# A fused retention and SoLU kernel with another written order: where each step stands in the queues, and which engine does it

## The chip, the cores and the metric

The kernel runs on one core of one Trainium2 chip. The time is the device time of one execution in microseconds (us), lower is better. The core has five instruction queues that run side by side: PE (TensorE, matrix products; its weight loads are shown as PEld), DVE (VectorE), ACT (ScalarE), POOL (GpSimd) and SP (SyncE, which here only issues DMA transfers). Each takes its instructions in the order in which they were written, and waits where an operand or a buffer is not ready.

## The reference

Per batch element and head, a causal product with decay (no softmax), and then a feed-forward layer over the joined heads:

```python
# q, k, v: 8 batch elements, 8 heads, 576 tokens, 64 wide, float32
scores = q @ k.T / 8
ret    = scores * gamma_h ** (i - j)         # for i >= j, otherwise 0
x      = (ret @ v), heads joined             # 4608 tokens x 512
h      = x @ w_in                            # 512 -> 1024
e      = exp(h - max(h));  sm = e / sum(e)
solu   = h * sm
ln     = (solu - mean(solu)) / sqrt(var(solu) + 1e-6) * g_ln
out    = ln @ w_out                          # 1024 -> 512
```

## The kernel before, in words

The 4608 tokens are cut into 36 chunks of 128 tokens, in four groups of nine; a group covers two batch elements, with chunks 0, 2, 4, 6 of one, 1, 3, 5, 7 of the other, and a ninth that holds the last 64 tokens of both. Within a batch element a running state (64 x 64 per head) goes from chunk to chunk.

The decay is split into factors of the row and of the column. A chunk runs through these steps (names as in the code):

- `lq`, `lk`, `lv`: SyncE issues loads of 256 KB each (profile lines L271 and L275).
- `cq`, `ck`, `cv`: scale or cast to f16 (tiles q, k, v), on GpSimd, VectorE or ScalarE.
- `tq`: PE transposes q and k into the PSUM tile tp; `eq` copies it to qkT (ScalarE or VectorE, L246). Late chunks use DMA transposes (`kd`, `kq`) instead, in part.
- `sc`: PE makes the scores (L392); `mk`: VectorE masks them into ret (L405).
- `av`, `fs`: PE makes x from ret and v, and adds the state's part (L467, L259); `ex` copies it to xT.
- `kv`: PE makes the chunk's state product kp (L416); `ad`: VectorE adds it to the state, t (L431); `dk`, `d3`: GpSimd scales the state for the next chunk (L443, L455).
- `m1` (`mr` by blocks, for the first two chunks): PE multiplies with w_in into h (L259). `mx`: VectorE's maximum (L523). `xp`: ScalarE's exponential, with its sum. `so`: VectorE's product u (L538), with its sum. For the first five chunks `ce` subtracts the mean.
- `sq`: ScalarE's squares (L564, L566); `ra`, `rp`: the factor rs of the row, small operations.
- `tu`: PE transposes u into lp, `eu` copies it to uT; or `du`, a DMA transpose. `m2`: PE multiplies with w_out into o (L259). `st`: ScalarE scales o by rs, and SyncE stores it.

Beside the chunks: `li` loads a quarter of w_in (512 KB), `wi` casts half a quarter; `lo` loads a quarter of w_out, `wo` scales an eighth by g_ln; `mm` multiplies with ones for the mean of w_out over its rows (tile mean), `mc` copies it into the tile warm, and eight steps `ws` subtract it from w_out, into w_c (L832). From the sixth chunk on `m2` uses w_c in place of w_out, so that `ce` is not needed. `wu` is a filler product on PE whose result nobody reads. The last chunk goes by halves (`hm`, `hx`, `hp`, `ho`, `ht`, `he`, `hq`, `h2`, `hw`).

No scheduler orders the work. A table of 1027 tokens, ORDER, is the program's order: a token `cq:7:v` is the step cq of chunk 7 on VectorE (a is ScalarE, g GpSimd). Each queue gets its instructions in this order. Two more tables, BANKS and SLOTS, say which PSUM bank and which SBUF buffer each step takes; there are four banks beside the two buffers of h, so a step of PE also waits for the reader of what stood in its bank:

```python
    def bank(shape, dtype, name):
        return ps.tile(shape, dtype, tag="b" + next(banks), name=name)
...
    def ws(c, e):
        ENG[e].tensor_tensor(out=T["w_c"][:, c], in0=w_out16[:, c], in1=warm, op=ALU.subtract)
...
    def run(order, base):

        for token in order.split():
            name, n, *more = token.split(":")
...
                step[name](n, *more)
```

Of the kernel before, what the change touches and what calls it, by code (L numbers as in the profile page):

```python
# [19 lines left out]

PLAIN = 5
ORDER = """
c1:0 lk:1 lk:0 lq:1 ck:0:v lq:0 cq:1:g lv:1 gt:0 lq:2 ck:1:v li:2 lv:0 cq:2:g cq:0:v tq:1 lk:2
cv:0:g lv:2 c2:0 tq:0 eq:1:av ck:2:a eq:0:v sc:1 li:0 cv:1:g wu:4:2 li:3 mk:1 li:1 wi:2:0:g lq:4
lv:4 lk:4 kv:0 wi:2:1:a lq:3 ad:0 sc:0 lk:3 cv:2:g tq:2 lv:3 eq:2:a av:1 mk:0 ex:1:a kv:1 ad:1
d3:0 av:0 ex:0:v sc:2 wi:0:0:a mr:1:2 dk:1 wi:0:1:g kv:2 mk:2 ad:2 wi:3:1:v wi:3:0:a mr:0:2
wi:1:1:v dk:0 wi:1:0:a lk:5 lq:5 mr:0:0 mr:1:0 mr:1:3 dk:2 mr:1:1 cq:4:g mx:1 mr:0:1 av:2 fs:2
ck:4:g mr:0:3 cv:4:g ex:2:a cq:3:g tq:4 mx:0 d3:1 xp:1 so:1 d3:2 wu:1:3 ce:1 wu:5:4 cv:3:g ck:5:g
eq:4:a cq:5:g sc:4 ck:3:a m1:2 xp:0 lv:5 mk:4 kv:4 tq:3 sq:1 kv:3 lk:6 lq:6 av:4 lv:6 so:0 ad:3
ra:1:g dk:3 ad:4 eq:3:a fs:4 tu:1 sc:3 ex:4:a ce:0 eu:1:a tq:5 d3:4 lo:0 cv:5:g lo:2 rp:1 lo:3  # L30
mx:2 eq:5:a xp:2 lo:1 cq:6:g m1:4 lv:8 mk:3 wu:2:1 ck:6:a cv:6:g tu:0 mx:4 sc:5 av:3 mk:5 eu:0:a
xp:4 fs:3 av:5 tq:6 kv:5 so:2 ex:3:a wo:0:a wo:1:g fs:5 kv:6 lk:8 m1:3 so:4 ce:2 eq:6:a ad:6
wo:4:g lq:7 lq:8 ex:5:a tu:2 sc:6 lk:7 m1:5 wo:6:g ce:4 mk:6 lq:13 wo:7:g wo:5:a d3:3 tu:4 lv:7
eu:2:a wo:2:a av:6 dk:6 wo:3:a mm:0 sq:2 dk:4 cv:8:g sq:4 mx:3 lq:9 eu:4:v m2:0 fs:6 ad:5 sq:0
ck:8:a mx:5 ra:0:v cq:7:v ra:2:v lv:13 mc:0:v lk:11 ck:7:v lq:12 lk:9 lv:10 m2:1 xp:3 lv:9 rp:0
cq:8:g so:3 ws:2:g lq:10 lk:10 ce:3 lq:11 ex:6:a st:0 lv:11 dk:5 ra:4:g st:1 ws:4:v rp:2 lv:16
ws:1:v lv:12 lk:13 tq:7 lk:12 tq:8 m2:2 eq:7:a eq:8:a sc:7 mk:7 xp:5 m1:6 so:5 st:2 rp:4 tu:3
sc:8 m2:4 sq:3 ra:3:v cv:7:g ck:11:a eu:3:a mk:8 cq:9:g av:7 fs:7 ws:7:g d3:5 ck:9:a lq:16 mx:6
kv:7 sq:5 cq:13:g rp:3 m2:3 ex:7:a lv:14 lq:15 ad:7 dk:7 ra:5:v tq:9 ws:5:g ws:3:g st:4 tu:5 m1:7
rp:5 ck:10:g av:8 ws:0:v cv:9:g xp:6 ws:6:v eu:5:a eq:9:va sc:9 so:6 mx:7 st:3 fs:8 ex:8:a m2:5  # L40
lq:21 tu:6 cq:11:g mk:9 cv:11:g m1:8 sq:6 av:9 st:5 cq:10:v kv:9 xp:7 ex:9:a tq:10 cq:12:g eu:6:v
so:7 ad:9 mx:8 eq:10:a ra:6:g cv:10:g sq:7 lq:24 m2:6 sc:10 lk:14 lq:14 xp:8 tu:7 mk:10 m1:9 rp:6
av:10 eu:7:v so:8 kv:10 st:6 ck:12:g ad:10 dk:9 ra:7:g tq:11 mx:9 ex:10:a ck:13:g tq:12 lq:18
tu:8 cv:14:g eq:11:av d3:9 eq:12:a lv:18 m2:7 sq:8 cv:12:g eu:8:a rp:7 sc:11 st:7 ra:8:v lk:16
mk:11 xp:9 lk:15 m1:10 lk:17 kv:11 ad:11 dk:10 av:11 so:9 lq:20 cq:21:g d3:10 kv:12 fs:11 ck:14:a
ad:12 m2:8 lk:18 mx:10 sc:12 lv:15 lk:20 lv:21 rp:8 ex:11:a cq:14:g lq:17 lk:22 tu:9 m1:11 mk:12
cq:16:g sq:9 xp:10 cq:15:g ra:9:v lv:19 st:8 tq:13 eq:13:a eu:9:v av:12 fs:12 tq:14 eq:14:a rp:9
dk:11 so:10 mx:11 m2:9 d3:12 cv:13:g tu:10 ex:12:a sc:13 m1:12 mk:13 st:9 av:13 sc:14 sq:10
eu:10:v xp:11 dk:12 fs:13 mx:12 ex:13:a so:11 xp:12 sq:11 mk:14 m2:10 ra:10:g lv:17 so:12 kv:14
rp:10 m1:13 st:10 ad:14 ck:18:g kv:13 tu:11 d3:11 eu:11:a av:14 ck:16:g ck:15:g ad:13 fs:14 tq:16  # L50
ra:11:v tq:15 du:12 lk:19 cv:16:g cq:17:g rp:11 d3:14 ex:14:a lk:21 d3:13 cv:15:g dk:13 lq:23
lv:24 m2:11 mx:13 dk:14 eq:15:av cv:18:g ck:17:v xp:13 lq:19 sc:15 mk:15 m1:14 eq:16:a av:15
# [36 lines left out]
ht:35:1 he:35:1:v ht:35:0 rp:34 m2:34 he:35:0:v hq:35:1:a rp:33 st:33 ra:35:v h2:35:0 st:34
h2:35:1 rp:35 hw:35:0:a hw:35:1:v  # L90
"""

BANKS = """
0123012031202310231032103021302310321023032031023102103120213120312031201203123031023013021320120312
0312032312013213012312301231302130312032131021301301032012301230130231031201320213021302130231023103
123120123301230103023012103102301320120
# [7 lines left out]
kf 012345102345102345012034513204153240  # L104
qf 012345601234560132564350136405126043
k16 012345012354012543021304532104203451
q16 012340213402134123012301324103104201
vf 012345610234561045301265410365240531
h 010101010101010101010101010101010101
v16 012341023410324012431042301342043120  # L110
qkT 012301230123102310231203120320231023
ret0 012301230123012301230123012301230123
ret1 012301230123012301230123012301230123
t 01230123102310320132013201323012
xT 012301230123012301230123012301230123
s32 0123012301230132013201302
s16 012312032013201320132013201232013
e 01201201201201201201201201201201201
u 01234023140231402314023142013421031
uT 01234102341023410234012340123401230  # L120
o_sb 01230123012301230123012301230123012
"""

# [753 lines left out]
```

## Time and profile before

| | |
|---|---|
| median of 3 runs | 211.23 us (211.11 to 211.67) |
| the profiled execution | 213.29 us |
| its span, from first to last instruction | 211.6 us |
| PE busy | 193.3 us (91%), 3109 matmuls |
| DVE, ACT, POOL busy | 173.3, 169.7, 170.6 us (82%, 80%, 81%) |
| chain that ended last | PE 70%, DMA 10%, issue on SP's queue 8%, DVE 5% |
| DMA | 47.97 MB, mean 227 GB/s |

Busy time on PE is what the profile models from the pipelined matmuls. The chain is followed back from the last instruction, at each step to what released it. A row of waits gives the waiting engine and tile, what it waited for, the sum in us, the count and the longest. A row of the timeline has the start, the length, the engine, line, operation and tiles, and in brackets the idle time ahead of it.

### The profile page before, as it was taken

What the parts mean: (1) busy time and instruction counts of PE and PEld (TensorE: products, weight loads), DVE (VectorE), ACT (ScalarE), POOL (GpSimd) and SP (SyncE); (2) the same over time, 40 slices, a digit from 0 to 9 for tenths busy, and PEclk for the clock granted to TensorE, in tenths of its full rate; (3) what the DMA queues carried; (4) which work ended last, traced back from release to release, by engine and by line L of the source; (5) the groups of instructions that cost most, each with busy time, mean ns of one, the idle gap of its engine ahead of it and who ended that gap; (6) DMA issues with size and microseconds to landing.
All of it is one profiled execution on the core that took longest, in us unless ns stands there. A gap on an engine that the chain in (4) does not pass through costs nothing.

```text
span 211.6 us, 7571 instructions
## 1 busy us (share of the span) xinstructions
PE 193.3 (91%) x3109; PEld 122.1 (58%) x3109; DVE 173.3 (82%) x299; ACT 169.7 (80%) x299; POOL 170.6 (81%) x249
## 2 busy tenths in 40 slices
PE   0468898888999999999999999999999999999992
PEld 0344576555666756676566666667656656555552
DVE  0468999849998969798989898999998999878640
ACT  2135889499988889889699899889989796799861
POOL 3379798679999999869999998789999987378330
PEclk9999999999999999999999999999999999999999
DMA  6999999979798998999999999989999999999734
GB/s 147 308 261 290 239 238 332 229 168 246 177 279 218 303 316 220 213 252 191 266 198 252 242 271 218 228 227 243 197 199 240 201 217 175 173 224 222 183 117 149
DMA packets 111890, 47.97 MB, mean 227 GB/s; under 512 B 95592, under 2 KB 105840, under 8 KB 111856
## 3 DMA queue, kind: packets, MB, share of 16 engines
q1 hardware_dynamic: 111536, 47.33, 97.1%
q8 instruction: 24, 0.39, 0.8%
q10 hardware_dynamic: 320, 0.16, 0.3%
q14 instruction: 10, 0.08, 0.1%
HBM read 32.54 MB, written 9.44 MB: 198 GB/s over the span
## 4 chain that ended last, share of the span: by engine, by line
PE 70%; DMA 10%; SPq 8%; DVE 5%; ACT 3%; issue 2%; POOL 0%; DVEq 0%; ACTq 0%
PE o L259 25%; PE h L259 22%; DMA w_out<-in_moe_w_out_dram 5%; PE tp L254 5%; PE sc L392 4%; SPq L275 3%; DMA w_in<-in_moe_w_in_dram 3%; PE x L259 3%; PE x L467 3%; PE lp L254 3%; SPq L271 2%; DMA vf<-in_v_dram 2%; ACT sq L564 2%; PE kp L416 1%; SPq L800 1%
## 5 line engine op out<-in xcount | busy, mean ns | idle before, releaser
L259 PE MATMUL h<-w_in,xT 128*64 128x512 f16 x560 | 67.3, 380 | 0.5 <-ACT w_in L246 0.3
L259 PE MATMUL o<-w_c,uT 128*64 128x512 f16 x480 | 56.5, 380 | 0.0
L405 DVE TENSOR_TENSOR ret<-sc,tris 128x512 f16<-128x512 f32 x72 | 46.1, 682 | 4.9 <-PE sc L392 4.7
L259 PEld LDWEIGHTS <-xT 128*64 128x64 f16 x576 | 31.0, 110 | 24.6 <-issue 1.4
L523 DVE TENSOR_REDUCE nm<-h 128x1 f32<-128x1024 f32 x35 | 42.5, 1217 | 2.8 <-PE h L259 2.5
L538 DVE SCALAR_TENSOR_TENSOR u<-h,e 128x1024 f16<-128x1024 f32 x35 | 42.5, 1216 | 2.0 <-ACT e L529 1.6
L259 PEld LDWEIGHTS <-uT 128*64 128x64 f16 x560 | 30.4, 111 | 22.6
L529 ACT ACTIVATE e<-h,nm 128x1024 f32<-128x1024 f32 x35 | 39.4, 1127 | 2.1 <-DVE nm L523 1.9
L289 POOL TENSOR_TENSOR v<-vf,small 128x512 f16<-128x512 f32 x34 | 35.4, 1044 | 5.4 <-DMA vf<-in_v_dram 5.3
L300 POOL TENSOR_TENSOR q<-qf,small 128x512 f16<-128x512 f32 x31 | 32.7, 1059 | 7.9 <-DMA qf<-in_q_dram 7.6
L566 ACT ACTIVATE sq<-u,su 128x1024 bf16<-128x1024 f16 x30 | 34.7, 1156 | 0.4 <-DVE u L538 0.2
L443 POOL TENSOR_TENSOR s<-t,small 128x512 f16<-128x512 f32 x32 | 33.5, 1055 | 0.2
L246 ACT COPY qkT<-tp 128x512 f16<-128x512 f16 x46 | 24.7, 595 | 8.4 <-PE tp L254 8.3
L626 ACT ACTIVATE o_sb<-o,rs 128x512 f32<-128x512 f32 x35 | 24.0, 696 | 7.6 <-POOL rs L592 2.3
L246 ACT CAST xT<-x 128x512 f16<-128x512 f32 x31 | 18.3, 594 | 6.6 <-PE x L259 4.9
L592 POOL TENSOR_TENSOR rs<-w,mhalf 128x1 f32<-128x1 f32 x36 | 20.6, 578 | 2.7 <-DVE w L581 1.5
L455 POOL TENSOR_TENSOR s<-t,small 128x256 f32<-128x256 f32 x24 | 15.5, 650 | 1.2 <-DVE t L431 1.1
L467 PE MATMUL x<-ret,v 128*64 128x128 f16 x288 | 14.7, 225 | 1.1 <-DVE ret L405 0.7
L254 PE MATMUL tp<-ident,q 128*64 128x128 f16 x232 | 12.2, 230 | 3.5 <-POOL q L300 3.2
L392 PE MATMUL sc<-qkT 64*128 64x128 f16 x288 | 14.9, 226 | 0.4 <-DVE qkT L246 0.3
L467 PEld LDWEIGHTS <-v 128*64 128x64 f16 x288 | 11.3, 113 | 5.3 <-issue 1.0
L254 PEld LDWEIGHTS <-q 128*64 128x64 f16 x280 | 10.8, 115 | 6.0 <-POOL q L300 3.3
(87 smaller groups left out, 263.1 us busy)
## 6 DMA issues: line engine op xcount, KB each, us to landing
kf<-in_k_dram SPq DMA_DIRECT2D x36, 256.0 KB, 5.2
qf<-in_q_dram SPq DMA_DIRECT2D x36, 256.0 KB, 4.8
vf<-in_v_dram SPq DMA_DIRECT2D x36, 256.0 KB, 5.2
out_dram<-o_sb SPq DMA_DIRECT2D x35, 256.0 KB, 4.2
w_in<-in_moe_w_in_dram SPq DMA_DIRECT2D x4, 512.0 KB, 6.1
w_out<-in_moe_w_out_dram SPq DMA_DIRECT2D x4, 512.0 KB, 8.5
uT<-u SPq DMA_TRANSPOSE x17, 4.4
out_dram<-o_sbh SPq DMA_DIRECT2D x2, 64.0 KB, 1.9
```

The lines of the kernel that those rows point to most:

```text
L246: (engine.copy if engine is nc.scalar else engine.tensor_copy)(out=out, in_=in_)
L254: nc.tensor.transpose(out=out[w], in_=in_[:, w], identity=ident)
L259: nc.tensor.matmul(out=out[w], lhsT=lhsT[:, w], rhs=rhs, start=start, stop=stop, skip_group_check=True,)
L289: engine.tensor_tensor(out=dst, in0=T.pop((key, n)), in1=table.unsqueeze(2).to_broadcast([P, H, D]), op=ALU.mult,)
L300: ENG[e].tensor_tensor(out=dst.rearrange("p (a h) d -> p h a d", h=2), in0=T.pop(("qf", n)).rearrange("p (h a) d -> p h a d", h=2), in1=ta ...
L405: nc.vector.tensor_tensor(out=r, in0=s, in1=m, op=ALU.mult)
L443: nc.gpsimd.tensor_tensor(out=s16, in0=t.unsqueeze(2).to_broadcast([P, 4, 2, D]), in1=gd.unsqueeze(3).to_broadcast([P, 4, 2, D]), op=ALU.mult,
L467: nc.tensor.matmul(out=x[64 * e : 64 * e + 64, hp], lhsT=v16[:, 2 * hp + e], rhs=ret[e][:, hp], start=hp == 0, stop=chunks[n][1] == 0, ski ...
L523: nc.vector.tensor_reduce(out=nm, in_=T["h", n], axis=AX.X, op=ALU.max, negate=True)
L529: nc.scalar.activation(out=e, in_=T["h", n], func=ACT.Exp, bias=T.pop(("nm", n)), accum_out=s)
L538: nc.vector.scalar_tensor_tensor(out=u, in0=T.pop(("h", n)), scalar=-1.0, in1=T.pop(("e", n)), op0=ALU.mult, op1=ALU.mult, accum_out=su,)
L566: nc.scalar.activation(out=s, in_=T.pop(("v", n)), func=ACT.Square, scale=-float(DFF), bias=T.pop(("su", n)), accum_out=ss,)
```

## The change

No function is changed. The three tables are replaced: the same 1027 steps in another order, with other banks and buffers. All 36 chunks keep their path (the same transposes by PE and by DMA). A step may stand on another engine: k's cast is ScalarE's for 19 chunks instead of 13, VectorE's for 3 instead of 6 and GpSimd's for 14 instead of 17; ws is VectorE's seven times instead of four and GpSimd's once instead of four times; half blocks of w_in are cast by ScalarE (4) and GpSimd (4, before 2 and VectorE 2). Chunk 7's q and k are scaled by GpSimd instead of VectorE. The fillers on PE are 13 products instead of 10, most of them ahead of the first product with w_in. One line of ORDER, before and after (the other lines, and the two smaller tables, differ in the same manner):

```diff
-c1:0 lk:1 lk:0 lq:1 ck:0:v lq:0 cq:1:g lv:1 gt:0 lq:2 ck:1:v li:2 lv:0 cq:2:g cq:0:v tq:1 lk:2
+c1:0 lk:1 ck:1:a lq:1 cq:1:g lk:0 lq:0 lq:2 lv:1 cq:0:v tq:1 li:2 lk:2 ck:0:a lv:0 li:0 ck:2:g
```

Three places show what moved. The first is SyncE's queue from the start; kf, qf and vf are loads of k, q and v of a chunk, w_in the loads of w_in. Before:

```order
L275 DMA kf<-in_k_dram 128x8x64 x2
L271 DMA qf<-in_q_dram 128x2x256 x2
L275 DMA vf<-in_v_dram 128x8x64
L271 DMA qf<-in_q_dram 128x2x256
L790 DMA w_in_94<-in_moe_w_in_dram 128x1024
L275 DMA vf<-in_v_dram 128x8x64
L275 DMA kf<-in_k_dram 128x8x64
L275 DMA vf<-in_v_dram 128x8x64
L790 DMA w_in_94<-in_moe_w_in_dram 128x1024 x3
```

After:

```order
L275 DMA kf<-in_k_dram 128x8x64
L271 DMA qf<-in_q_dram 128x2x256
L275 DMA kf<-in_k_dram 128x8x64
L271 DMA qf<-in_q_dram 128x2x256 x2
L275 DMA vf<-in_v_dram 128x8x64
L790 DMA w_in_94<-in_moe_w_in_dram 128x1024
L275 DMA kf<-in_k_dram 128x8x64
L275 DMA vf<-in_v_dram 128x8x64
L790 DMA w_in_94<-in_moe_w_in_dram 128x1024 x2
L275 DMA vf<-in_v_dram 128x8x64
L790 DMA w_in_94<-in_moe_w_in_dram 128x1024
```

The first q goes ahead of the second k, and two of w_in's blocks go ahead of chunk 2's v; the last block is thirteenth in both. Chunks 4, 3, 5 and 6 and then w_out follow in both.

The second place is ScalarE's queue where the last of w_out is scaled (w_out16 from w_out32 and g32), with the squares sq of chunks 0, 2 and 4 and the copy uT of chunk 2. Before:

```order
L246 COPY uT_915<-lp_836 128x1024
L808 ACTIVATE w_out16_97<-w_out32_95,g32_93 128x512 x2
L564 ACTIVATE sq_947,ss_948<-u_775 128x1024
L564 ACTIVATE sq_954,ss_955<-u_818 128x1024
L564 ACTIVATE sq_990,ss_991<-u_560 128x1024
```

After:

```order
L564 ACTIVATE sq_810,ss_811<-u_527 128x1024
L808 ACTIVATE w_out16_97<-w_out32_95,g32_93 128x512 x3
L564 ACTIVATE sq_905,ss_906<-u_777 128x1024
L564 ACTIVATE sq_1008,ss_1009<-u_786 128x1024
L246 COPY uT_1011<-lp_908 128x1024
```

One square goes ahead of the scaling and the copy uT goes behind the other two. The second output product of PE now takes the PSUM bank of the tile lp that this copy reads.

The third place is VectorE's queue at the subtractions w_c (steps `ws`). Before:

```order
L554 TENSOR_SCALAR u_1047<-u_1047,nmu_1055 128x1024
L832 TENSOR_TENSOR w_c_1010<-w_out16_97,warm_89 128x512 x2
L405 TENSOR_TENSOR ret0_1155<-sc0_1145,tris_86 128x512
...
L523 TENSOR_REDUCE nm_1274<-h_1162 128x1
L431 TENSOR_TENSOR t_1315<-kp_1276,s32_1268 128x256
L577 TENSOR_SCALAR w1_1319<-s_1160 128x1
L583 TENSOR_SCALAR w2_1320<-ss_1286,w1_1319 128x1
L832 TENSOR_TENSOR w_c_1010<-w_out16_97,warm_89 128x512 x2
```

After:

```order
L832 TENSOR_TENSOR w_c_1016<-w_out16_97,warm_89 128x512
L549 TENSOR_SCALAR nmu_1147<-su_1103 128x1
L554 TENSOR_SCALAR u_1102<-u_1102,nmu_1147 128x1024
L405 TENSOR_TENSOR ret0_1214<-sc0_1162,tris_86 128x512
...
L523 TENSOR_REDUCE nm_1235<-h_1177 128x1
L832 TENSOR_TENSOR w_c_1016<-w_out16_97,warm_89 128x512 x4
L431 TENSOR_TENSOR t_1367<-kp_1298,s32_1160 128x256
L832 TENSOR_TENSOR w_c_1016<-w_out16_97,warm_89 128x512
L246 COPY uT_1390<-lp_1331 128x1024
```

Four of the subtractions stand between chunk 6's maximum nm and the state sum t of chunk 7, which was ahead of them, and a fifth ahead of the copy uT of chunk 5.

More of the change, by code (lines that the diff above doesn't have):

```diff
@@ L29 @@
[L29 to L40, printed above, removed]
@@ new lines @@
+kv:6 wo:5:a lq:7 m1:3 wo:2:a wo:6:g wo:3:a ad:5 sc:6 wo:7:g m1:5 ce:4 mk:6 ad:6 tu:4 lk:8 dk:4
+sq:2 tu:2 eu:4:v av:6 cv:8:g lq:9 mx:3 lk:7 lq:8 dk:6 lq:13 lv:7 ra:0:v ra:2:v lk:10 lk:9 m2:0
+lv:9 lv:10 mm:0 rp:0 lq:12 cq:7:g sq:4 eu:2:a ck:8:a mc:0:v st:0 mx:5 lk:11 m2:1 lq:10 lk:13
+ck:7:g lv:12 fs:6 cq:8:g rp:2 xp:3 ws:3:g st:1 ws:2:v cv:7:g dk:5 tq:7 lv:13 ex:6:a lk:12 lq:11
+lv:16 lv:11 so:3 ra:4:g eq:7:a m2:2 ws:6:v tq:8 ce:3 xp:5 rp:4 cq:9:g st:2 d3:5 sc:7 eq:8:a
+ck:9:a m1:6 sq:3 tu:3 mk:7 sc:8 so:5 mk:8 mx:6 eu:3:a ws:4:v m2:4 ws:0:v av:7 fs:7 st:4 lv:14
@@ new lines @@
+sc:11 m1:10 mk:11 rp:7 kv:11 d3:10 av:11 ra:8:g rp:8 ad:12 lq:16 fs:11 so:9 ad:11 st:7 ck:14:a
+cq:13:g ck:13:g mx:10 lk:17 ex:11:a lv:19 m2:8 lv:15 dk:11 sq:9 lk:15 st:8 sc:12 lk:20 mk:12
+cq:14:g tu:9 ra:9:v dk:10 lk:22 cq:18:g m1:11 xp:10 tq:13 eu:9:v tq:14 av:12 fs:12 cq:15:g
+eq:13:a lq:17 rp:9 so:10 ex:12:v eq:14:av m2:9 sc:13 lv:21 tu:10 mx:11 mk:13 eu:10:v m1:12 av:13
+sq:10 fs:13 xp:11 d3:12 sc:14 d3:11 so:11 ra:10:g st:9 ck:16:a ex:13:a cq:21:g lv:24 ck:18:g
+cq:16:g mx:12 sq:11 m2:10 kv:14 dk:12 mk:14 lq:23 ad:14 xp:12 so:12 m1:13 ck:15:g tu:11 rp:10
@@ new lines @@
+du:12 cv:15:g lv:17 ra:11:g lq:19 kv:13 st:10 ad:13 d3:14 d3:13 tq:15 lk:21 lk:19 eu:11:a av:14
+mx:13 fs:14 eq:15:av tq:16 ex:14:a m2:11 sq:12 sc:15 dk:13 eq:16:v mk:15 rp:11 xp:13 m1:14
+ck:17:g cq:17:g so:13 av:15 fs:15 cq:23:g st:11 ex:15:a dk:14 kv:15 tq:17 tu:13 sq:13 ad:15 sc:16
+eq:17:a m1:15 mx:14 mk:16 kv:16 xp:14 ra:13:v av:16 eu:13:a fs:16 cv:19:g ex:16:a m2:12 ad:16
+so:14 dk:15 sq:14 dk:16 lv:20 du:14 mx:15 sc:17 lq:20 lk:24 cv:17:g rp:13 m2:13 lv:23 lv:22
+ra:14:g mk:17 xp:15 lq:22 st:13 ck:20:v ra:12:g so:15 tq:18 ck:21:g lk:23 rp:12 rp:14 eq:18:av
@@ new lines @@
+ck:19:a m1:16 cv:18:g av:17 mx:16 st:12 sq:15 xp:16 sc:18 mk:18 so:16 du:16 lk:28 lk:29 lq:25
+fs:17 m2:14 ex:17:a tu:15 st:14 ra:15:v lq:32 cq:19:g tq:19 kv:18 eq:19:a ad:18 m1:17 lq:27
+cq:20:g eu:15:v cv:24:g av:18 mx:17 sc:19 sq:16 m2:15 ex:18:a ck:22:a ck:24:g xp:17 mk:19 kv:19
+tq:20 tq:21 lq:26 rp:15 so:17 eq:20:av cv:21:g cq:22:g m1:18 ad:19 eq:21:av cv:20:g mx:18 cv:23:g
+lk:25 av:19 st:15 sq:17 ex:19:a sc:20 mk:20 xp:18 lq:28 lk:26 so:18 m2:16 tu:17 ck:28:a kv:20
+av:20 ra:16:g du:18 rp:16 eu:17:a dk:18 d3:18 fs:20 st:16 cv:22:g lv:25 ra:17:v lv:26 ck:23:v
@@ new lines @@
+dk:31 av:31 xp:30 d3:30 cv:32:g fs:31 mk:32 lq:35 kq:34 dk:30 d3:31 lv:35 so:30 m1:29 ex:31:a
+cv:33:g du:28 sc:33 kv:32 mk:33 ad:32 m1:31 av:32 st:25 fs:32 av:33 fs:33 mx:29 kv:33 ra:26:g
+mx:31 ex:32:v m2:26 sq:30 d3:32 ex:33:a ra:30:g rp:26 ad:33 xp:29 xp:31 so:29 du:29 dk:32 st:26
+so:31 ck:35:a cv:34:g cq:35:g sq:28 m2:27 sc:34 ra:28:g m1:32 sq:31 ra:31:g mk:34 mx:32 tq:35
+xp:32 av:34 fs:34 rp:28 ra:27:v eq:35:a kv:34 du:31 ad:34 so:32 du:32 ex:34:a m1:33 m2:28 sq:32
+mx:33 cv:35:v sc:35 m1:34 du:30 dk:34 mk:35 rp:27 st:28 sq:29 dk:33 ra:29:g xp:33 mx:34 xp:34
@@ L96 @@
-123120123301230103023012103102301320120
+0123012031201203131202310232103201231032132013013201203201321230123013203201302131320132013210210321
+0230123023120230213213203210123012102310213021301320132013021320120321023102310123012301203213120123
+012030312012013203120122012010321320120
 """
@@ L103 @@
 SLOTS = """
[L104 to L108, printed above, removed]
+kf 012345012354012534120531425310243125
+k16 012345012354012350412043501240123450
+qf 012345601234560215643216043216041526
+q16 012340123401234012341340342012340143
+vf 012345601234560132650416243051624350
+qkT 012301230123012301230213021302310231
+v16 012341023410321421342034130142301423
 h 010101010101010101010101010101010101
-v16 012341023410324012431042301342043120
-qkT 012301230123102310231203120320231023
 ret0 012301230123012301230123012301230123
 ret1 012301230123012301230123012301230123
-t 01230123102310320132013201323012
 xT 012301230123012301230123012301230123
-s32 0123012301230132013201302
-s16 012312032013201320132013201232013
+t 01230210312031021302130231023102
+s16 012301230213012301230123012032102
+s32 0123012031023120312031230
 e 01201201201201201201201201201201201
-u 01234023140231402314023142013421031
-uT 01234102341023410234012340123401230
+u 01234012340123401234012340132401321
+uT 01234103241032413024312041320143201
 o_sb 01230123012301230123012301230123012
```

94 lines of the change are left out of this document (37 added, 57 removed).

## The prediction

> **What bounds the kernel now.** I first read the busy time by stage, five stretches that I chose where the character of the trace changes.
>
> ```profile
> core 0: us, PE busy (x) PEld busy (x) DVE busy (x) ACT busy (x) POOL busy (x), PEclk, DMA share, GB/s
> 0.00:20.00 20.00, 9.99 (x137) 6.83 (x138) 10.03 (x21) 6.22 (x10) 11.60 (x23) 1.00 0.97 258
> 20.00:44.00 24.00, 20.40 (x366) 13.60 (x367) 21.60 (x36) 18.50 (x33) 19.99 (x25) 1.00 0.95 246
> 44.00:62.00 18.00, 17.46 (x259) 10.90 (x256) 15.12 (x32) 17.59 (x33) 16.45 (x19) 1.00 0.89 217
> 62.00:180.00 118.00, 118.00 (x2010) 74.99 (x2010) 107.81 (x178) 104.24 (x184) 107.91 (x155) 1.00 1.06 232
> 180.00:208.00 28.00, 27.42 (x348) 15.77 (x342) 18.37 (x36) 23.14 (x44) 14.62 (x31) 1.00 0.86 186
> ```
>
> From 62 to 180 us PE never stops (118.00 of 118.00), so nothing can be won there. An order alone can win only PE's idle time ahead of 62 us and in the last stretch, and can lose anywhere. The steps of PE have the same work in both orders except for three more filler products (below). The waits of PE, for 8 to 50 us and then from 50 us on, say which idle time it is.
>
> ```profile
> PE tp L254 <- POOL q L300: 3.2, 1, 3.2
> PE kp L416 <- POOL v L289: 1.7, 1, 1.7
> PE mean L259 <- ACT w_out L808: 1.7, 2, 1.5
> ...
> PE tp L254 <- DVE k L246: 0.4, 1, 0.4
> ...
> PE tp L254 <- DVE warm L246: 0.2, 1, 0.2
> ...
> PE x L467 <- POOL v L289: 0.4, 1, 0.4
> ```
>
> The first two lie ahead of 14 us. What they cost is read from the chain that ended last.
>
> ```profile
> 12.55 6.92 DMA w_in<-in_moe_w_in_dram
> ...
> 31.20 10.99 DMA w_out<-in_moe_w_out_dram
> ...
> 42.84 0.71 ACT w_out L808
> ...
> 45.80 1.16 ACT sq L564 x2
> ```
>
> Two landings pace the ramp: the last block of w_in (12.55 + 6.92 = 19.47 us) and the last block of w_out (31.20 + 10.99 = 42.19 us), which is scaled by 43.55 us. The DMA share of 0.95 to 0.97 says that the queue is full until then. So idle time of PE ahead of 42 us is bought back only if w_out lands earlier. Behind 43.55 us the time up to 62 us counts one for one, because PE is saturated from there to the end.
>
> **The change part by part.**
>
> *The first 42 us.* SyncE's row has the same 21 loads and 4 blocks of w_in ahead of w_out in both orders. w_in's second to fourth blocks go from places 11, 12, 13 to 10, 11, 13: the last one keeps its place, so I leave 19.47 and 42.19 us as they are. Chunk 1's q is loaded second instead of third, and its transposes should start about a microsecond earlier; that is worth nothing while w_in lands at 19.47. The three more fillers fall into the wait ahead of 14 us and cost nothing; uncovered, six matmuls in pairs would cost 3 x 0.22 = 0.7 us (sixteen take 1.73 us, next fence).
>
> GpSimd now casts half of the last block of w_in, and behind that wait stand two scalings of chunk 2's state and chunk 4's q.
>
> ```profile
> 20.44 1.08 POOL L300 TENSOR_TENSOR q<-qf,small 128x512 f16<-128x512 f32 x1
> ...
> 40.92 0.60 PE L259 MATMUL mean<-w_out,ones 128*64 128x512 f16 x4
> 40.94 0.68 DVE L246 COPY uT<-lp 128x1024 f16<-128x1024 f16 x1
> ```
>
> The q, at 20.44 us before, then starts at about 19.5 + 0.6 + 1.05 + 0.65 = 21.8 us, 1.3 us later. The cover is the wait for w_out: VectorE and PE had done this stage's work by 41.6 us, ahead of 42.19, and PE could use nothing before 43.55. Without that cover it costs up to 1.3 us.
>
> *42 to 62 us.* These rows of the timeline and of the chain carry the next sum.
>
> ```profile
> 43.60 1.27 PE L259 MATMUL mean<-w_out,ones 128*64 128x512 f16 x10 [0.21 <-ACT w_out L808]
> ...
> 52.02 0.40 PE L392 MATMUL sc<-qkT 64*128 64x128 f16 x8
> ...
> 61.65 0.39 PE L467 MATMUL x<-ret,v 128*64 128x128 f16 x8
> 38.31 1.02 ACT L246 COPY uT<-lp 128x1024 f16<-128x1024 f16 x1
> 42.22 1.33 ACT L808 ACTIVATE w_out<-w_out,g 128x512 f16<-128x512 f32 x2 [2.89 <-DMA w_out<-in_moe_w_out_dram]
> 50.09 2.06 ACT L246 COPY qkT<-tp 128x512 f16<-128x512 f16 x4
> 57.12 0.22 PE x L259 x8
> 57.47 1.73 PE o L259 x16
> 59.19 0.45 PE tp L254 x16
> ```
>
> Before, PE runs the rest of the mean, two output products, chunk 6's state product and 7's transposes, and stops for warm and for k of chunk 7, both VectorE's. After, both scalings of chunk 7 are GpSimd's, ahead of which stands no wait on the mean. In exchange the copy uT of chunk 2 (38.31 us, in the gap before w_out) moves behind two squares, and the second output product takes over the PSUM bank that this copy empties. By hand: five pairs of the first output product are left at 43.60 (10/16 of 1.73 = 1.08), then the mean, 46.41 us. The copy starts after two squares, at 45.80, and ends 1.02 later: 46.82, a new wait of 0.4. Then o 1.73, state 0.22, transposes 0.45, o 1.73, transposes 0.45: PE stands before the scores of chunk 7 at 51.40 us, against 52.02. The scores need ScalarE's copies of chunk 7: the same ScalarE work but a 1.02 us copy for a 1.16 us square, so half of the 2.06 us row, 51.12 less 0.14, is 50.98. In time, by 0.4. **Term: -0.6 us**, with bounds of -0.1 (only ScalarE's 0.14, since it is busy 17.59 of 18 us and would pace everything) and -0.6.
>
> *VectorE's subtractions.* Seven of the eight subtractions of the mean from w_out are VectorE's now instead of four. The rows of the tile w_c, and what follows them:
>
> ```profile
> L832 POOL TENSOR_TENSOR w_c<-w_out,warm x4: 1151/1242/1337, 49.1 to 61.1; 128x512 f16<-128x512 f16 x4
> L832 DVE TENSOR_TENSOR w_c<-w_out,warm x4: 408/414/1267, 51.7 to 58.9; 128x512 f16<-128x512 f16 x4
> 56.64 1.21 DVE L523 TENSOR_REDUCE nm<-h 128x1 f32<-128x1024 f32 x1
> L431 DVE TENSOR_TENSOR t<-kp,s 128x256 f32<-128x256 f32 x24 | 9.8, 419 | 3.3 <-POOL s L455 1.8 <-PE kp L416 1.0 <-POOL k L246 0.2
> L443 POOL TENSOR_TENSOR s<-t,small 128x512 f16<-128x512 f32 x32 | 33.5, 1055 | 0.2
> L246 DVE COPY uT<-lp 128x1024 f16<-128x1024 f16 x7 | 4.8, 682 | 0.2 <-PE lp L254 0.2
> ```
>
> Four of them now stand in a row between chunk 6's reduction and the state sum t of chunk 7, then a fifth and the copy uT of chunk 5. The reduction ends at 56.64 + 1.21 = 57.85, less about 0.9 for the earlier start (0.6, and two small operations that left VectorE): I take 56.9. With w us for one subtraction, t ends at 56.9 + 4w + 0.42, and GpSimd's scaling s at 56.9 + 4w + 1.48. PE wants s right behind chunk 8's product x, 61.65 - 0.6 + 0.2 = 61.25, and the bank under uT behind that, near 61.5. So w may be 0.72. At 0.41 (median) there is over a microsecond of room and the term is **zero**; at 1.27, uT ends at 56.9 + 5 x 1.27 + 0.42 + 0.68 = 64.35 and PE waits 2.9 us. I take 0.41, as the median row has it and as GpSimd, waiting for t, should be idle beside four of the five.
>
> The longest of the four took three times the median with GpSimd busy in that stretch. The Trainium skill ("SBUF — State Buffer", Who interferes with whom) says that a VectorE operation with two SBUF inputs and a GpSimd operation that reads SBUF exclude one another for the whole instruction. The 1267 ns agree with that, the 408 ns show that it need not happen; it is the first rival below, and speaks against this change.
>
> *The late stretch.* One stop of PE is left there.
>
> ```profile
> 182.35 3.91 DMA vf<-in_v_dram
> 186.33 1.05 POOL v L289
> 187.43 0.41 PE L467 MATMUL x<-ret,v 128*64 128x128 f16 x8 [0.35 <-POOL v L289]
> ```
>
> Chunk 34's v is issued at 182.35 and PE waits for its scaling. In the new order its load stands some 14 us of PE work ahead of its scaling, counted from the durations above, where it stood 8. **Term: -0.4 us**; next late is chunk 35's q, whose load keeps about 7 us, more than the 3.91.
>
> *Everything else.* ScalarE has six more casts of k and fewer halves of qkT, GpSimd three fewer casts.
>
> ```profile
> L246 ACT CAST k<-kf 128x512 f16<-128x512 f32 x13 | 8.3, 635 | 4.3 <-DMA kf<-in_k_dram 4.3
> ```
>
> 6 x 0.635 = 3.8 us more on ScalarE, about 3 of them between 62 and 180 us, where it has 13.8 us free. I price that at zero: PE's order is nearly the same there, with the same work between a transpose and its scores to within a microsecond or two. The bounds are 0 and +3.
>
> **The sum.** -0.6 - 0.4 = -1.0 us against the profiled execution's own 213.29 us (span 211.6 and 1.7 around it), so 212.3 there. The median of the runs shown, 211.23, is 2.1 us below that execution; I take the same -1.0 off it: **210.2 us**.
>
> **The rivals.** A measurement of this kernel can tell about 0.3%, 0.63 us, from no change.
>
> *The subtractions are held up by GpSimd.* Place: 57 to 62 us. It decides from 0.72 us for one on the mean; the four before had a mean near 0.63. At 1.27 PE loses 2.9 us: 211.23 - 1.0 + 2.9 = 213.1, slower. For it: one of four did take 1.27. Against: GpSimd has less to do there. Named in the skill's rule above.
>
> *ScalarE paces 42 to 62 us.* It is busy 17.59 of 18 us. Then only 0.1 is won there, with 0.4 at the end: 210.7, within 0.3%. The same result comes if w_in's shift, which is one or two places in the queue, is all that the change does at the front.
>
> *ScalarE paces the steady stretch.* If half of its 3 us reaches PE, 211.23 - 1.0 + 1.5 = 211.7, and at all of it 213.2. Against: 13.8 us free.
>
> *w_out lands sooner.* The new mixture of the loads would have to move the same bytes faster. PE's 1.7 us wait goes as well: 208.5. Against: a queue that is full.
>
> **Chances.** Forecast 0.36, w_out sooner 0.08: faster 0.44. ScalarE paces the ramp, or small new waits eat the gain: same 0.29. Subtractions held up 0.16, ScalarE in the steady stretch or another new wait 0.11: slower 0.27. The range from 208.8 to 213.0 leaves out most of the two extreme prices and holds the rest.
>
> **What would show it.** Right: PE's first scores behind w_out near 51.4 us, no wait for warm or k there, a short new wait of o for uT; seven subtractions near 0.41 us; no stop near 187 us; the end of the last matmul 1 us earlier. Wrong: subtractions over 0.72 us and PE waiting for s or uT near 61 us; waits of PE on ScalarE behind 62 us; a landing of w_out away from 42.2 us, which would mean that the front is not paced by the same bytes as I take it.

## The result, and the profile after

| | before | after |
|---|---|---|
| median | 211.45 us (211.11 to 211.94, 4 runs) | 209.09 us (208.82 to 209.76, 4 runs) |
| ratio | | 0.9891 (95% interval 0.9859 to 0.9923) |
| the profiled execution | 213.29 us, span 211.6 | 209.08 us, span 207.4 |

The changed kernel is faster by 2.4 us, where the forecast said 1.0. The profiled executions of before (1.8 us above its median), and below of `b0_again`, `a_again` and `a_best`, were slow ones, so that a part of the 4.2 us between the two spans is not the change's, and the ratios compare fast executions only.

The busy time by stage of the kernel after, in the stretches and columns of the forecast's first fence:

```profile
0.00:20.00 20.00, 12.52 (x159) 7.17 (x161) 9.91 (x20) 7.49 (x12) 9.39 (x22) 1.00 0.99 263
20.00:44.00 24.00, 21.32 (x378) 14.19 (x376) 22.71 (x40) 21.57 (x39) 22.82 (x28) 1.00 1.09 265
44.00:62.00 18.00, 18.00 (x296) 11.65 (x293) 16.42 (x31) 17.04 (x32) 15.60 (x22) 1.00 1.00 232
62.00:180.00 118.00, 117.45 (x1996) 73.80 (x1992) 107.75 (x181) 106.45 (x188) 105.92 (x147) 1.00 1.14 232
```

PE is busy 3.4 us more by 44 us (33.84 against 30.39) and has no idle time left from 44 to 62. The waits of PE after, first from 8 to 50 us (the longest two), then from 50 us to the end (all of them):

```profile
PE tp L254 <- POOL q L300: 1.2, 1, 1.2
PE tp L254 <- DVE ret L405: 0.6, 1, 0.6
...
PE sc L392 <- DMA qkT<-q: 0.6, 1, 0.6
```

The stops for `mean` behind w_out, for warm and for k are gone, and of those for v two of 0.2 us are left. A new one stands at 179.7 us, ahead of the scores of chunk 34. These rows of the timeline answer to those of the forecast's 42 to 62 us:

```profile
39.17 1.33 ACT L808 ACTIVATE w_out<-w_out,g 128x512 f16<-128x512 f32 x2 [0.73 <-DMA w_out<-in_moe_w_out_dram]
...
39.88 1.95 PE L259 MATMUL o<-w_out,uT 128*64 128x512 f16 x16
...
48.39 0.40 PE L392 MATMUL sc<-qkT 64*128 64x128 f16 x8
...
59.10 1.92 PE L259 MATMUL o<-w_c,uT 128*64 128x512 f16 x16
```

The last block of w_out is scaled from 39.17 us, 3.05 us sooner than in the profile before, and the scores of chunk 7 start at 48.39, against 52.02 before and 51.40 in the forecast. And the subtractions w_c:

```profile
L832 DVE TENSOR_TENSOR w_c<-w_out,warm x7: 415/418/764, 45.3 to 56.0; 128x512 f16<-128x512 f16 x7
L832 POOL TENSOR_TENSOR w_c<-w_out,warm x1: 1217/1217/1217, 48.0 to 48.0; 128x512 f16<-128x512 f16 x1
```

### The profile page after: what moved, and what is told of

Read it like the earlier page. It is cut to its first block, busy times and chain, and to the rows that moved or that the text cites. A ratio compares the mean times of both kernels' runs of the same rounds, so it can differ in the third digit from the quotient of the medians.

```text
span 207.4 us, 7573 instructions
## 1 busy us (share of the span) xinstructions
PE 192.9 (93%) x3115; PEld 120.7 (58%) x3115; DVE 174.0 (84%) x306; ACT 172.3 (83%) x305; POOL 162.6 (78%) x236
## 4 chain that ended last, share of the span: by engine, by line
PE 71%; DVE 7%; DMA 6%; SPq 6%; POOL 5%; ACT 2%; issue 2%; DVEq 0%; POOLq 0%
PE o L259 26%; PE h L259 22%; PE tp L254 5%; PE sc L392 4%; DMA qf<-in_q_dram 4%; PE lp L254 3%; PE x L467 3%; PE x L259 3%; DMA qkT<-q 2%; SPq L790 2%; DVE ret L405 2%; SPq L275 2%; POOL v L289 2%; PE kp L416 2%; DVE u L538 1%
## 5 line engine op out<-in xcount | busy, mean ns | idle before, releaser
L259 PEld LDWEIGHTS <-xT 128*64 128x64 f16 x576 | 30.5, 110 | 23.3 <-issue 0.2
L289 POOL TENSOR_TENSOR v<-vf,small 128x512 f16<-128x512 f32 x33 | 34.3, 1043 | 0.4 <-DMA vf<-in_v_dram 0.4
L246 ACT COPY qkT<-tp 128x512 f16<-128x512 f16 x44 | 23.8, 601 | 10.3 <-PE tp L254 10.3
L592 POOL TENSOR_TENSOR rs<-w,mhalf 128x1 f32<-128x1 f32 x36 | 21.4, 600 | 9.0 <-DVE w L583 8.1
L246 ACT CAST xT<-x 128x512 f16<-128x512 f32 x32 | 18.9, 595 | 5.0 <-PE x L259 4.6
L254 PE MATMUL tp<-ident,q 128*64 128x128 f16 x232 | 11.9, 226 | 8.8 <-POOL q L300 8.0
L455 POOL TENSOR_TENSOR s<-t,small 128x256 f32<-128x256 f32 x24 | 14.6, 613 | 0.6 <-DVE t L431 0.2
L246 ACT CAST k<-kf 128x512 f16<-128x512 f32 x19 | 12.0, 632 | 3.2 <-DMA kf<-in_k_dram 3.2
```

Of the source, the lines that this page charges most:

```text
L246: (engine.copy if engine is nc.scalar else engine.tensor_copy)(out=out, in_=in_)
L254: nc.tensor.transpose(out=out[w], in_=in_[:, w], identity=ident)
L259: nc.tensor.matmul(out=out[w], lhsT=lhsT[:, w], rhs=rhs, start=start, stop=stop, skip_group_check=True,)
L289: engine.tensor_tensor(out=dst, in0=T.pop((key, n)), in1=table.unsqueeze(2).to_broadcast([P, H, D]), op=ALU.mult,)
```

## The experiments

Twelve runs on three chips; each ratio is to the kernel before, run between them on the same chip. In each text on record, A and B are that text's own. The theory to begin with (A): the long profile of before hides what paces its front; in an ordinary execution w_out lands sooner than 42 us, PE is late itself, and the changed front is worth its own time. The rival (B): the new order of the loads makes w_out land sooner. The marks of all the profiles, start times in us, in one table:

| kernel | scores of chunk 4 | scores of chunk 7 | first product with w_c | span | ratio (95% interval) |
|---|---|---|---|---|---|
| before, profile shown | 25.21 | 52.02 | 62.74 | 211.6 | |
| b0_again | 25.55 | 50.16 | 60.87 | 211.0 | 0.9994 (0.9943 to 1.0044) |
| b_loads | 25.88 | 50.34 | 61.05 | 210.5 | 1.0004 (0.9966 to 1.0042) |
| b_loads_fill | 26.35 | 50.96 | 61.67 | 211.4 | 1.0001 (0.9958 to 1.0045) |
| b_loads_kv | 26.92 | 52.29 | 63.00 | 212.5 | 1.0065 (1.0023 to 1.0107) |
| b_front | 24.09 | 48.41 | 60.34 | 210.7 | 1.0011 (0.9962 to 1.0060) |
| after | 24.05 | 48.39 | 59.10 | 207.4 | 0.9891 (0.9859 to 0.9923) |
| a_again | 24.66 | 48.59 | 59.31 | 210.2 | 0.9936 (0.9885 to 0.9987) |
| a_loads | 25.81 | 50.29 | 61.09 | 209.3 | 0.9955 (0.9920 to 0.9991) |
| a_ws | 24.04 | 47.99 | 60.00 | 209.0 | 1.0012 (0.9973 to 1.0051) |
| a_fill | 23.97 | 48.12 | 58.84 | 208.3 | 0.9927 (0.9872 to 0.9982) |
| a_kq | 24.10 | 48.40 | 59.12 | 206.7 | 0.9897 (0.9831 to 0.9963) |
| a_kq2 | 24.20 | 48.56 | 59.27 | 207.9 | 0.9931 (0.9889 to 0.9972) |
| a_best | 24.81 | 49.67 | 60.38 | 212.8 | 0.9903 (0.9857 to 0.9948) |

### What paces the front: b0_again, b_loads, a_loads

`b0_again` is the kernel before, unaltered.

> The kernel before once more, unchanged, for a second profile. Theory A (the profile of before that the prediction used, 213.29 us against a median of 211.4, was a late one: its landing of w_out at 42.2 us is about 2 us later than usual): w_out's last block lands at 40 to 41 us here, and the execution takes about 211.3. Theory B (the order of the loads itself makes w_out land 3 us sooner in the kernel after): w_out lands at 42 us again, within 0.5 us, whatever the execution's total.

The timeline of this second profile:

```profile
40.31 1.33 ACT L808 ACTIVATE w_out<-w_out,g 128x512 f16<-128x512 f32 x2
...
42.04 1.89 PE L259 MATMUL mean<-w_out,ones 128*64 128x512 f16 x16
...
50.16 0.40 PE L392 MATMUL sc<-qkT 64*128 64x128 f16 x8
```

No bracket stands behind the first two rows: w_out was there when ScalarE came to it, scaled by 41.64, and PE came to the mean at 42.04 without waiting for it. The same holds in `b_loads`, where ScalarE starts at 40.49 us. In the forecast's profile ScalarE stood 2.89 us for that block. That landing was one execution's, and A holds: the work ahead of w_out, not its landing, sets the scores of chunk 7, at 50.2 to 50.3 us. A's 211.3 us for the execution was missed: the profiled one took 212.76, though w_out was in time.

`b_loads` is the kernel before with only its first 29 transfers reordered as the changed kernel has them; `a_loads` is the changed kernel with the first 29 as before.

```diff
 the loads, ORDER of before (-) and after (+)
-lk:1 lk:0 lq:1 lq:0 lv:1 lq:2 li:2 lv:0 lk:2 lv:2 li:0 li:3 li:1 lq:4 lv:4 lk:4
+lk:1 lq:1 lk:0 lq:0 lq:2 lv:1 li:2 lk:2 lv:0 li:0 li:1 lv:2 li:3 lk:4 lq:4 lv:4
```

> The kernel before with one part of the change: SyncE issues the first 29 transfers (21 loads, 4 blocks of w_in, 4 of w_out) in the order of the kernel after; every engine's own order, the banks and each chunk's buffers stay as before. Theory B: w_out lands 1 to 3 us sooner than in the kernel before and the time falls by 1 to 2 us (ratio 0.990 to 0.995). Theory A, and the step of the prediction that the same bytes land at the same time: landing and time as before, within 0.3%. Theory C (the gain sits in PE's and ScalarE's order behind w_out): as before too, perhaps slower by up to 1 us where the old order meets loads that come in another sequence.

> The kernel after with one part undone: the first 29 transfers in the order of the kernel before, all else as after. Theory B: w_out lands 1 to 3 us later than in the kernel after, and 1 to 2 us of the gain are lost (209.1 becomes 210 to 211). Theories A and C: 209.1 us, within 0.6.

B falls: the load order alone gives nothing (ratio 1.0004, scores of chunk 7 at 50.34). But without it the changed kernel's front gives nothing either: in `a_loads` the scores of chunk 4 are back at 25.81 and those of chunk 7 at 50.29. (B's loss of 1 to 2 us came, though not by w_out, for which ScalarE does not wait there.) The 0.45% that `a_loads` still wins lies behind: from the scores of chunk 7 to the end it takes 159.0 us, `b_loads` 160.2, and 1.0 of that is the difference of one stop for a transposing transfer in the late stretch (0.5 against 1.5). Why each half is lost shows in the waits of PE in `b_loads`, in GpSimd's timeline of `b0_again`, and in ScalarE's and PE's of `a_loads`:

```profile
PE kp L416 <- POOL v L289: 3.5, 1, 3.5
```

```profile
23.03 0.61 POOL L246 CAST k<-kf 128x512 f16<-128x512 f32 x1 [1.63 <-DMA kf<-in_k_dram]
```

```profile
19.23 0.62 ACT L246 CAST w_in<-w_in 128x512 f16<-128x512 f32 x1 [2.81 <-DMA w_in<-in_moe_w_in_dram]
...
20.38 0.32 PE L416 MATMUL kp<-v,k 128*64 128x64 f16 x8 [0.95 <-ACT xT L246]
```

Before, chunk 4's k is the sixteenth transfer and GpSimd waits for it until 23 us, PE 1.2 us behind it; in the new order it is the fourteenth, and in `b_loads` that wait is gone. But the v of chunk 0 goes from place 8 to place 9, and in the old order of products PE has `kv:0` ahead of everything else there. In `a_loads` it is a block of w_in, `li:1`: thirteenth in the old order of loads, eleventh in the new. The new order of ScalarE casts it ahead of a copy xT, so that ScalarE stands 2.81 us for the block and PE 0.95 us for the copy.

### Which half of the front: b_loads_fill, a_fill, b_loads_kv, b_front

```diff
 b_loads_fill, against b_loads
-wu:4:2
+wu:4:7
 a_fill, against after
-wu:2:4 ... wu:4:3
+wu:2:1 ... wu:4:1
```

> The kernel before with the changed kernel's first 29 loads, and 14 filler products in place of 4 after the first score products (wu:4:2 becomes wu:4:7). Theory A (in the stretch up to 25 us the changed kernel wins by two things together: chunk 4's q and k land sooner, and TensorE, kept busy by fillers from 9.8 us on, runs its 128x128 products at the short duration from 13.5 us instead of 17 us): the score products of chunk 4 start at 24.5 to 24.9 us instead of 25.9, and the ratio to the kernel before is 0.994 to 0.996. Theory B (the win comes from the castings, which the changed kernel moves from GpSimd to VectorE in this stretch; load order and fillers alone give nothing): the score products of chunk 4 stay at 25.5 to 26 us, ratio 0.999 to 1.001.

> The changed kernel with 4 filler products instead of 14 between the first two score products (wu:2:4 wu:4:3 become wu:2:1 wu:4:1). Theory A (the fillers buy the short product duration early): the products between 13 and 17 us take the long duration, and the score products of chunk 4 start 0.5 to 1.2 us later than the changed kernel's 24.05, ratio to it 1.002 to 1.006. Theory B (TensorE waits 1.2 us for the q of chunk 4 just ahead of them, which swallows the slower products, so that the fillers do nothing): chunk 4 within 0.2 us of 24.05, ratio to the changed kernel 1.000.

Both went against A (and 26.35 in `b_loads_fill` is later than its B's 26 too). With ten more filler matmuls the old front stands still for v (1.9 us) and then for w_in; with ten fewer, the new one starts chunk 4 at 23.97. The waits of PE in `b_loads_fill`, and then in `a_fill`:

```profile
PE kp L416 <- POOL v L289: 1.9, 1, 1.9
PE h L259 <- POOL w_in L246: 1.0, 1, 1.0
```

```profile
PE tp L254 <- POOL q L300: 1.4, 1, 1.4
```

The wait for chunk 4's q, 1.2 us in the changed kernel, takes what the fillers change. `b_loads_kv` moves the first products as well:

```diff
 b_loads_kv, against b_loads (steps between are left out; a few banks change too)
-kv:0 ... ad:0 sc:0 ... av:1 mk:0 ex:1:a kv:1 ad:1 d3:0 av:0 ... sc:2
+sc:0 cv:1:v mk:0 kv:1 ... av:1 kv:0 ex:1:a av:0 ad:0 ... sc:2 ad:1 d3:0
```

> The kernel before with the changed kernel's first 29 loads, as in b_loads, and with the first products of chunks 0 and 1 in the changed kernel's order: sc:0 ahead of kv:1, kv:1 and av:1 ahead of kv:0, the v of chunk 1 scaled by VectorE, ad:0, ad:1, d3:0 and mk:0 placed to suit. Theory A (with the new load order the v of chunk 0 is cast about 1 us later, and TensorE stood 3.5 us for it with the score products of chunk 0 behind; the load order pays only if nothing stands behind that v): the stop for v shrinks to under 1.5 us, the score products of chunk 4 start at 24.2 to 25.0 us instead of 25.9, ratio to the kernel before 0.993 to 0.997. Theory B (chunk 4 is set by its own q, k and by GpSimd's later work): chunk 4 stays at 25.5 to 26 us, ratio 0.999 to 1.001.

The stop for v went, and VectorE, which now has one v more, became late in its place; the kernel is slower than before, 1.0065. A fell again. Its waits of PE:

```profile
PE kp L416 <- DVE ret L405: 1.2, 1, 1.2
PE tp L254 <- DVE q L300: 0.7, 1, 0.7
PE sc L392 <- DVE xT L246: 0.6, 1, 0.6
```

So no single piece was found that carries the front's gain; loads, products and the engine of each casting go together. `b_front` takes them all: the first 173 steps of the changed kernel, up to `sc:6`, then what is left of the kernel before in its order.

> The kernel before whose first 173 steps, up to the score products of chunk 6, are the changed kernel's, in its order, with its loads, fillers and choice of engines, and its banks; behind them every step of the kernel before that is then still to be done, in its own order, the subtractions of the w_out means as it has them. Theory A (the gain arises in this front, where the score products of chunk 7 come at 50.2 to 51 us in the kernel before and at 48.0 to 48.6 in the changed one): they come at 48.2 to 48.8 us, ratio to the kernel before 0.990 to 0.993. Theory B (the gain arises behind it, in the later order and on VectorE): ratio 0.997 to 1.001, with the front's gain spent again in waits on w_out or on GpSimd before 62 us.

The scores of chunk 7 come at 48.41, as in the changed kernel (48.39), though the old order stands behind those of chunk 6; and the ratio is 1.0011. The front's gain was there and was lost. Where, its timeline shows:

```profile
55.13 2.53 DVE L832 TENSOR_TENSOR w_c<-w_out,warm 128x512 f16<-128x512 f16 x2
57.58 0.68 DVE L246 COPY qkT<-tp 128x512 f16<-128x512 f16 x1
...
56.04 2.63 POOL L832 TENSOR_TENSOR w_c<-w_out,warm 128x512 f16<-128x512 f16 x2
...
58.94 0.40 PE L392 MATMUL sc<-qkT 64*128 64x128 f16 x8 [0.52 <-ACT qkT L246]
...
60.34 1.92 PE L259 MATMUL o<-w_c,uT 128*64 128x512 f16 x16 [0.43 <-ACT o_sb L626]
```

Two subtractions on VectorE took 2.53 us while GpSimd was at work, at first on a state scaling and then on two more subtractions; the copy of chunk 9's qkT stood behind them, then ScalarE's copy, then PE. In `b0_again` the same two took 1.60 us. Of the lead of 1.75 us on `b0_again`, 0.53 was left at the first product with w_c. By the table, PE takes 10.7 to 10.8 us from the scores of chunk 7 to that product in all the other profiles, with the old order as with the new, but 11.9 in `b_front` and 12.0 in `a_ws` (next). (The order behind the cut was not made for this front, so that a small part may be the joint.)

### Whose subtractions: a_ws

```diff
-ws:2:v ws:5:v ws:7:v
+ws:2:g ws:5:g ws:7:g
```

> The kernel after with the subtractions of blocks 2, 5 and 7 back on GpSimd (four on each engine), everything else as after. By the prediction's step on the subtractions VectorE has slack there (seven at 0.41 us fit ahead of PE's need), so 209.1 us within 0.3%, with GpSimd about 2.5 us busier. By the rival, that VectorE and GpSimd hold one another up, it would be faster than after by up to 1 us. By a third view, that GpSimd is the one that is short behind w_out, slower by up to 1.5 us.

The gain went, ratio 1.0012: of the three views on record the third holds, that GpSimd is short. The tile w_c, then PE's and GpSimd's timeline:

```profile
L832 DVE TENSOR_TENSOR w_c<-w_out,warm x4: 422/673/1371, 46.6 to 54.6; 128x512 f16<-128x512 f16 x4
L832 POOL TENSOR_TENSOR w_c<-w_out,warm x4: 1153/1241/1341, 47.0 to 56.9; 128x512 f16<-128x512 f16 x4
```

```profile
56.95 1.15 POOL L832 TENSOR_TENSOR w_c<-w_out,warm 128x512 f16<-128x512 f16 x1
58.06 1.04 POOL L443 TENSOR_TENSOR s<-t,small 128x512 f16<-128x512 f32 x1
...
59.16 0.58 PE L259 MATMUL x<-qkT,s 128*64 128x64 f16 x14 [1.10 <-POOL s L443]
```

The state scaling s starts at 58.06 instead of 56.17 and PE stands 1.10 us for it. PE starts its first product with w_c 0.9 us later than in the profile after, though it was 0.4 ahead at chunk 7. That 0.9, and 0.5 more at the stop ahead of chunk 34 (1.1 against 0.6), make up most of the 1.6 us between the two spans. The ratio 1.0012 lies 1.6 us above that of `a_again` and 2.6 above that of the first series. But the profiled execution, 210.78 us, was the shortest of its twelve (their median is 212.62), so this reading does not price the whole loss, and where the rest arises is not shown.

The two rows of totals of this line in the grouped view, `a_ws` and then after, say why it pays:

```profile
L832 DVE TENSOR_TENSOR w_c<-w_out,warm 128x512 f16<-128x512 f16 x4 | 3.0, 785 | 0.0
```

```profile
L832 DVE TENSOR_TENSOR w_c<-w_out,warm 128x512 f16<-128x512 f16 x7 | 3.0, 467 | 0.0
```

Seven on VectorE cost it the same 3.0 us that four cost while GpSimd did the others. Beside `a_ws` the three were free, and took 3.7 us (3 x 1.24) off GpSimd. Over all the profiles seven cost VectorE 2.7 to 4.0 us, and four 2.3 or 2.4 with the old order and front and 3.3 in `b_front`.

### The late stop: a_again, a_kq, a_kq2, a_best

`a_again` is the changed kernel, unaltered, in a later series; in `a_kq` and `a_kq2` one transfer is issued earlier, and `a_best` exchanges the loads of chunk 4 as well.

```diff
 a_kq, against after
-lk:35 ... lq:35 kq:34
+kq:34 lk:35 ... lq:35
 a_best, against a_kq
-lk:4 lq:4
+lq:4 lk:4
```

> The changed kernel once more, unaltered, so that the kernels beside it can be read against it on the same chip. Both theories: 0.989 of the kernel before (0.986 to 0.992), the last w_out block landing between 38 and 40 us, the score products of chunk 7 at 48 to 49 us, one stop of about 0.6 us ahead of the score products of chunk 34.

> The changed kernel with the transposing transfer of chunk 34's q issued ahead of the two loads of chunk 35 instead of behind them. Theory A (the 0.55 us stop ahead of the score products of chunk 34 is the queue's: the q was cast at 168.1 us and its transfer was issued at 174.4, behind two loads): the stop goes, the time is 0.4 to 0.6 us shorter than the changed kernel's, ratio to the kernel before about 0.987. Rival (what is late next is as late: the u of a chunk, or the transfers themselves): the stop moves or stays, no difference.

> The kernel a_kq once more, beside the ones above: no stop ahead of the score products of chunk 34, ratio to the kernel before 0.985 to 0.990.

> The changed kernel with the transposing transfer of chunk 34's q ahead of the loads of chunk 35, as in a_kq, and with the loads of chunk 4 exchanged, q ahead of k. Theory A (the stop of 1.1 to 1.4 us ahead of chunk 4's q products is the landing of q, for which GpSimd stood 0.45 us): the stop is 0.4 us shorter, and the time 0.3 to 0.4 us below that of a_kq. Rival (the k of chunk 4, now the later one, takes its place, or landing doesn't follow the order of issue that closely): no difference from a_kq.

`a_again` came at 0.9936, outside the 0.986 to 0.992 expected. The stop ahead of the scores of chunk 34 was 0.55 us in the first profile, 1.7 in `a_again` (0.6 expected), 1.2 in `a_fill` and 1.1 in `a_ws`. With the transfer ahead of the loads it is gone in all three profiles; the busy time from 170 to 190 us, after and then `a_kq`:

```profile
170.00:190.00 20.00, 19.45 (x276) 11.16 (x274) 18.19 (x29) 16.39 (x30) 14.72 (x26) 1.00 0.98 193
```

```profile
170.00:190.00 20.00, 20.00 (x294) 11.64 (x292) 18.70 (x29) 17.00 (x30) 15.35 (x27) 1.00 0.96 187
```

The mechanism is shown; a gain in time is not. The intervals of 0.9897 (`a_kq`), 0.9931 (`a_kq2`, where 0.985 to 0.990 was expected) and 0.9936 (`a_again`) overlap, and in `a_kq2` the next in line, chunk 35's q on GpSimd, stopped PE for 0.8 us. In `a_best` PE waited 0.8 us for chunk 4's q, no other than in the two without that exchange (1.1 and 0.7), and the wait for its copy qkT grew from 0.3 to 0.8: nothing is won there, and its profile has other stops of 0.5 to 1.1 us from 91 us on. All three beat the kernel before; none is shown to beat the changed one.

## Why the forecast was right in its sign and too small

**Step 1, the first 42 us, failed.** It read the landing of w_out at 42.19 us from one execution and let it set the clock: "idle time of PE ahead of 42 us is bought back only if w_out lands earlier". In `b0_again`, `b_loads` and `b_loads_fill` ScalarE came to the last block at 40.3 to 41.2 us and did not wait for it. The forecast had named this sign of being wrong itself, a landing away from 42.2 us. So the front's own work counts, and its term was not 0 but about -1.5 us (scores of chunk 4 at 24.05 against 25.55); at chunk 7 the lead is 1.8 us (48.39 against 50.16), where 0.6 was forecast. In `a_again` the two leads are 0.9 and 1.6 us. The rival that w_out lands sooner had 208.5 us, nearer to 209.09 than the forecast's 210.2, but by luck: the new order of the loads, its cause, gains nothing alone (`b_loads`). Two details of the step were wrong too. "Chunks 4, 3, 5 and 6 ... follow in both" is true, but within chunk 4 the k moved up two places, and before it was the k that GpSimd waited for. And the q of chunk 4 did come later, at 21.14 instead of 20.18 to 20.44 us, as the step said; PE waited 1.2 us for it, uncovered, and was 1.5 us ahead nonetheless. The fillers cost nothing, as said: ten matmuls fewer changed chunk 4 by 0.1 us.

**Step 2, 42 to 62 us, -0.6, failed for the same reason.** Its moves were found: the second output product starts some 0.3 us late, just behind the copy uT (0.4 was worked out), and no wait for warm or k is left. But `b0_again` has no wait for warm or for k of chunk 7 either: they too stood in the one execution that the forecast read. And `b_front`, with the old order behind the scores of chunk 6, reaches those of chunk 7 at 48.41 us, the changed kernel at 48.39: behind the new front these moves are worth nothing up to there. The 1.2 of 1.75 us that `b_front` loses lie behind the scores of chunk 7, at the subtractions.

**Step 3, the subtractions, at 0.41 us each.** Right: 418 ns in the median, 467 on the mean, under the threshold of 720, and from the scores of chunk 7 to the first product with w_c PE takes 10.7 us before and after, so the term is zero. What the step left out is what the new front would lose if they stayed where they were: it asked only whether VectorE had room for three more, not what GpSimd would do with 3.7 us less. In `a_ws` that stretch is 1.3 us longer. The rival named a mechanism that is there, with the wrong sign: a subtraction on VectorE can be dear while GpSimd is at work, on a subtraction (up to 1371 ns in `a_ws`, in `b_front` two in 2.53 us) or on a scaling (1267 ns in before beside s, 1199 in `a_loads` beside q). The change makes such meetings rarer: the means are 415 to 599 ns in the seven profiles with seven on VectorE, 626 to 857 in the seven with four. The Trainium skill ("SBUF — State Buffer", Who interferes with whom) has VectorE operations with two SBUF inputs and GpSimd operations that read SBUF exclude one another; these means agree with that.

**Step 4, the late stretch, -0.4.** The stop for v went, as said. A stop of 0.5 to 1.7 us for the transposed q of chunk 34 came. Nor was the 0.4 of before typical: other profiles of its order stood 1.3 to 1.6 us there for a transposed u, or 1.0 for a transposed k. Over the profiles the late stretch gains a few tenths at most, and is not settled.

**Step 5, ScalarE, zero.** Right: PE has no wait for a cast of k behind 62 us in the profile after, with ScalarE at 106.45 of 118 us.

**The sum.** -1.0 became -2.4 in the first series and -1.4 in `a_again` (0.9936); the two intervals overlap, and the forecast's 0.995 lies outside the first and inside the second. The measured 209.09 us is at the lower edge of the forecast's range (208.8 to 213.0). Steps 1 and 2 were to bring 0.6 us up to the scores of chunk 7 and brought 1.8: that is 1.2 of the 1.4 us missing in the first series. The right sign owes something to luck: the -0.6 came from waits of one execution, and the gain from the part that was priced at nothing. What stays open is which of the front's pieces are needed, how much of the late stop is luck, and why `b_front` and `a_ws`, still 0.5 and 0.9 us ahead of `b0_again` at the first product with w_c, take no less time than before.

## What to carry to other kernels

A landing time read from one profile is a sample, not a bound: before you let it cover everything ahead of it, ask whether the engine that uses the data waits for it in a second profile. Gains in an ordered program come in sets: the front paid only with the new order and the moved subtractions behind it (`b_front`, `a_ws`), and three sets of its pieces without the rest gave 0, 0 and 0.65% more time. And when work goes from one engine to another, price it on both, along with what the two do to each other meanwhile.

## What the runs showed of the hardware

Transfers vary from one execution to the next by about as much as the change is worth: the last block of w_out was waited for until 42.2 us in one execution of the kernel before and was there by 40.3 in another, and the same transposing transfer of chunk 34's q stopped PE for 0.5 to 1.7 us.

The duration of PE's small products falls by more than a third in the ramp, though the granted clock is shown as 1.00 there: eight transposes of 128x128 take 0.64 us at first and 0.40 later. PE's timeline of after, then of `a_fill`:

```profile
8.54 0.63 PE L254 MATMUL tp<-ident,k 128*64 128x128 f16 x8
...
13.68 0.40 PE L254 MATMUL tp<-ident,q 128*64 128x128 f16 x8
```

```profile
13.13 0.69 PE L467 MATMUL x<-ret,v 128*64 128x128 f16 x8
...
15.75 0.40 PE L392 MATMUL sc<-qkT 64*128 64x128 f16 x8
```

With ten filler matmuls fewer the step came some 2 us later (the products at 14.55 us still took 0.64). It moves without any change too: in `a_again`, the same kernel as after, scores take 0.40 us from 11.95 on, where after's still take 0.61 at 12.98. And it can go back: in `b_loads_fill`, after PE's stop of 1.9 us for v, scores took 0.40 us at 14.83 and 0.61 again at 17.18, and here the granted clock is shown as 0.50 from 16 to 18.8 us. The Trainium skill ("TensorE: Matmul & The Clock Gate", Part 1) gives an array clock that doubles after about 3.4 us of steady work, which agrees with the kind of step, if not to the microsecond; here the sooner step was worth nothing, since PE then waited for q.
